# Loading one weight matrix row by row over the 16 DMA engines: a different split of w_out, and more of it on GpSimd's queue

## The chip, the cores and the metric

The kernel runs on one core of a Trainium2 chip. The metric is the device time of one execution in microseconds, the median of the runs shown. Lower is better. The core has a matrix engine (TensorE, "PE"), VectorE ("DVE"), ScalarE ("ACT"), GpSimd ("POOL") and SyncE ("SP"), and 16 DMA engines that carry every transfer between memory and the core's SBUF. [...]

## The reference

```
x  = A_x                                   # 4 tokens x 640, bf16
xn = layernorm(x)
# attention, one new token per batch entry, 32 heads of 128, cache of 4096 positions
q  = xn @ wq                               # 640 x 4096
p  = softmax(q . k_cache / sqrt(128))      # k_cache: 4 x 32 x 4096 x 128
A  = (p . v_cache) @ wo                    # 4096 x 640
# gMLP, F = 1728, so Fh = 864
z  = gelu(xn @ w_in)                       # 640 x 1728
z1 = z[:, :864];  z2 = layernorm(z[:, 864:])
B  = (z1 * (w_sp * z2 + b_sp)) @ w_out     # w_out: 864 x 640
out = x + A + B
```

The two caches hold 134 MB each; w_out holds 864 rows of 1280 bytes, 1.1 MB.

## The kernel before

**Attention.** The 32 heads are four groups of 8; with 4 batch entries there are 16 "units" of K and 16 of V, each 128 partitions x 65,536 bytes. All of them pass through one SBUF tile `kv` of five slots, each half a unit wide. `seq` (line 148) sets the order K0 K1 K2 K3 V0 K4 V1 K5 ... V15, `place` (154) the two slots of each unit, and `load_unit` (174) issues one transfer (two for a K unit that ends a group). SP issues them in that order (lines 181 and 189), each as soon as the slots that it overwrites have been read. K2, for instance, goes to slots 2 and 3; slot 3 holds the first half of K0 until it has been transposed.

For a K unit `emit_K` makes eight steps: VectorE transposes 128 x 2048 words from `kv` into `w_words` (line 425, two alternating buffers), and TensorE multiplies from there (436). After the fourth unit of a group there is a softmax; `emit_V` (503) multiplies a V unit (509).

**gMLP.** It runs while the first K unit is on its way. Of the 864 rows of w_out a part lies in `w_out`, a tile of 128 partitions x `FA` chunks of one row each, and the rest in `w_rest`, a view of `w_words` (line 129) with `FR` chunks, of which only some partitions are filled; VectorE zeroes it first (128). `PC` (61) lists the pieces of the rest: first and last partition, rows per partition, and k. `load_piece` (131) loads a piece with the source rows ordered so that its leading dimension has k entries. Pieces 0 and 1 are issued by SP (139, 140), piece 2 by POOL, behind a small transfer `walk` (141) whose data nobody uses; `tc.issue_after` (142) fixes that order. The columns of w_in are picked in the same order as the rows of w_out, so the z values land in the partition and chunk where their row of w_out lies (lines 317 to 361: matmuls into `z_ps` and `zr_ps`, then Gelu into `zT`). Then follow the layernorm, the gate and a transposition (to 390), and `FC = FA + FR` chunks x 2 halves of matmuls of line 403, which accumulate in `proj`. TensorE executes in program order, so its K matmuls stand behind those of line 403; and since `w_rest` and the buffers of line 425 are the same words, VectorE's first K transposition waits until line 403 has read them.

**The end.** After V15 come the last pieces of wo (189), the rest of the output projection (552) and two stores.

Of the kernel before, what the change touches and what calls it, by code (L numbers as in the profile page):

```python
# [1 line left out]

# [9 lines left out]
F32 = mybir.dt.float32  # L12
BF16 = mybir.dt.bfloat16
# [3 lines left out]
def kernel(  # L17
# [19 lines left out]
    nc = tc.nc  # L37
    P = 128
    B, Sq, D = A_x.shape
    _, H, Sk, Dh = A_k_cache.shape  # L40
    assert Sq == 1 and B == 4 and Dh == P and D % P == 0
    DC = D // P
# [11 lines left out]
    G = HG * B  # L54
    F2 = B_w_in.shape[1]
    Fh = F2 // 2
    FA = 3
    FR = 17
    nf = FA * P

    PC = ((0, 20, 10, 5), (32, 44, 12, 3), (60, 68, 17, 2))
    f_at = [nf]
    for p0, p1, n, _ in PC:
        f_at.append(f_at[-1] + (p1 - p0) * n)
    assert Fh == f_at[-1]
    FC = FA + FR
    NOUT = A_wo.shape[1]
# [5 lines left out]
    const = ctx.enter_context(tc.tile_pool(name="const", bufs=1))  # L73
# [5 lines left out]
    ps_o = ctx.enter_context(tc.tile_pool(name="ps_o", bufs=2, space=bass.MemoryType.PSUM))  # L79
# [6 lines left out]
    def misc_ps(shape, dtype):  # L86
        misc_ctr[0] += 1
        return ps_m.tile(shape, dtype, tag="misc", name=f"misc{misc_ctr[0]}")
# [5 lines left out]
    n_p = (2 * TC + 1) * 16  # L94
    w_words = const.tile([P, max(2 * NKT + n_p, FR * NOUT // 2)], F32, name="w_words")
    kT_t = w_words[:, 0:2 * NKT].rearrange("p (i n) -> p i n", i=2)
    pT_t = w_words[:, 2 * NKT:2 * NKT + n_p].bitcast(BF16).rearrange("p (j r) -> p j r", r=32)

    def at_slot(i, n, off=0):
        return kv[:, i * SL + off:i * SL + off + n]  # L100
# [22 lines left out]

    w_out = at_slot(2, FA * NOUT, n_in).rearrange("p (c n) -> p c n", c=FA)

    nc.sync.dma_start(out=w_out[:, 0:2], in_=B_w_out[0:2 * P, :].rearrange("(p c) n -> p c n", p=P))
    nc.sync.dma_start(out=w_out[:, 2:3], in_=B_w_out[2 * P:nf, :].rearrange("(p c) n -> p c n", p=P))
    nc.vector.memset(w_words[:, 0:FR * NOUT // 2], 0.0)  # L128
    w_rest = w_words[:, 0:FR * NOUT // 2].bitcast(BF16).rearrange("p (c n) -> p c n", c=FR)

    def load_piece(eng, t):
        p0, p1, n, k = PC[t]
        return eng.dma_start(out=w_rest[p0:p1, 0:n].rearrange("p c n -> p (c n)"),
                             in_=B_w_out[f_at[t]:f_at[t + 1], :].rearrange("(r i c) n -> i r (c n)", i=k, c=n))

    NST = 256
    walk = const.tile([14, NST], BF16)

    load_piece(nc.sync, 0)
    load_piece(nc.sync, 1)  # L140
    sw = nc.gpsimd.dma_start(out=walk, in_=B_w_out[0:14, 0:NST].rearrange("(r i) n -> i r n", i=7))
    with tc.issue_after(sw.ins):
        load_piece(nc.gpsimd, 2)

    NB = 32 * FC
    z_at = n_in + FA * NOUT

# [72 lines left out]
    xnT = const.tile([P, DC, 32], BF16)  # L220
# [43 lines left out]
    for q in range(4):  # L264
        nc.gpsimd.tensor_copy(out=SelE[32 * q:32 * q + 32, :, q % 2, :],
                              in_=b8[32 * q:32 * q + 32, 8:8 + HP, None].to_broadcast((32, HP, P // HG)))
# [10 lines left out]
                          in_=ident_f[:].rearrange("p (q x c) -> p q x c", q=2, c=C2))  # L277
# [12 lines left out]
    for hf in range(NH):  # L290
        nc.tensor.matmul(proj[0:32, 0:NO2], lhsT=ident_bf[:XR, 1 - hf:33 - hf],
                         rhs=x_bf[:, hf * NO2:(hf + 1) * NO2], start=(hf == 0), stop=False)
# [4 lines left out]
    for hf in range(2):  # L297
        for c in range(DC):
            for j in range(NG):
                n0 = j * HG * Dh + hf * 512  # L300
                nc.tensor.matmul(q4_ps[32 * j:32 * j + 32, hf * 512:hf * 512 + 512], lhsT=xnT[:, c, :],  # L301
                                 rhs=wq[:, c, n0:n0 + 512], start=(c == 0), stop=(c == DC - 1))
# [14 lines left out]
    w_z = w_in.rearrange("p c (a f) -> p c a f", a=2)  # L317
    z_ps = misc_ps([P, 2, FA, 32], F32)
    zr_ps = misc_ps([P, 2, 256], F32)


    z_in = [[], [], [], []]
    for t, (p0, p1, n, k) in enumerate(PC):
        src = w_z[:, :, :, f_at[t]:f_at[t + 1]]
        for q in range(p0 // 32, (p1 - 1) // 32 + 1):
            x0, x1 = max(p0, 32 * q), min(p1, 32 * q + 32)
            if x1 - x0 < p1 - p0:
                assert (x1 - x0) * k == p1 - p0
                src_q = src.rearrange("p d a (r i c) -> p d i a r c", i=k, c=n)[:, :, (x0 - p0) // (x1 - x0)]
            else:  # L330
                src_q = src
            z_in[q].append((t, x0 - 32 * q, x1 - 32 * q, src_q))
    z_of = [[sum((x1 - x0) * PC[t][2] for t, x0, x1, _ in z[:m]) for m in range(len(z) + 1)] for z in z_in]
    w_z2 = w_z[:, :, :, 0:2 * P].rearrange("p c a (q j i) -> p c q a i j", q=4, j=32)
    w_z1 = w_z[:, :, :, 2 * P:nf].rearrange("p c a (q j) -> p c q a j", q=4)
    for c in range(DC):
        for q in range(4):
            nc.tensor.matmul(z_ps[32 * q:32 * q + 32, :, 0:2], lhsT=xnT[:, c, :], rhs=w_z2[:, c, q], start=(c == 0), stop=False)
            nc.tensor.matmul(z_ps[32 * q:32 * q + 32, :, 2], lhsT=xnT[:, c, :], rhs=w_z1[:, c, q], start=False,
                             stop=(c == DC - 1))  # L340
        for q in range(4):
            for m, (_, _, _, src) in enumerate(z_in[q]):
                nc.tensor.matmul(zr_ps[32 * q:32 * q + 32, :, z_of[q][m]:z_of[q][m + 1]], lhsT=xnT[:, c, :], rhs=src[:, c],
                                 start=(c == 0 and m == 0), stop=(c == DC - 1 and m == len(z_in[q]) - 1))
    z_f = at_slot(2, 2 * 3 * NB, z_at).bitcast(F32).rearrange("p (a n) -> p a n", a=3)
    z_b = at_slot(2, 2 * NB, z_at + 6 * NB).rearrange("p (a n) -> p a n", a=2)
    zT = z_f[:, 0:2, :].rearrange("p a (i j) -> p a i j", j=32)
    nc.gpsimd.memset(z_f[:, 0:2, :], 0.0)
    nc.scalar.activation(out=zT[:, :, 0:FA, :], in_=z_ps[:], func=ACT.Gelu_apprx_tanh)
    for q in range(4):  # L350
        rows = slice(32 * q, 32 * q + 32)
        for m, (t, x0, x1, _) in enumerate(z_in[q]):
            p0, p1, n, k = PC[t]
            z = zr_ps[rows, :, z_of[q][m]:z_of[q][m + 1]]
            dst = zT[rows, :, FA:FA + n, x0:x1]
            if x1 - x0 < p1 - p0:
                nc.scalar.activation(out=dst, in_=z.rearrange("p a (x c) -> p a c x", c=n), func=ACT.Gelu_apprx_tanh)
            else:
                for a in range(2):
                    nc.scalar.activation(out=dst[:, a].rearrange("p c (i r) -> p c i r", i=k),  # L360
                                         in_=z[:, a].rearrange("p (r i c) -> p c i r", i=k, c=n), func=ACT.Gelu_apprx_tanh)
# [36 lines left out]
    for f0 in range(0, FC, 4):  # L398
        for hf in range(NH):
            for fc in range(f0, min(f0 + 4, FC)):  # L400
# [3 lines left out]
                                 rhs=(w_out[:, fc] if fc < FA else w_rest[:, fc - FA])[:, hf * NO2:(hf + 1) * NO2],  # L404
                                 start=(fc == 1 and hf == 0), stop=False)
# [156 lines left out]
    for i, item in enumerate(seq):  # L562
# [10 lines left out]
        g, b = divmod(u, B)  # L573
# [22 lines left out]
    for c, hf in ((0, 0), (1, 0), (0, 1), (1, 1), (2, 0), (2, 1)):  # L596
        p = min(c, 1)
# [49 lines left out]
```

## Time and profile before

| | us |
|---|---|
| median of 3 runs | 663.58 (663.44 to 665.17) |
| the profiled execution: its span | 661.8 |
| VectorE busy | 377.1 |
| TensorE busy (matmul) | 286.8 |
| ScalarE, GpSimd busy | 74.0, 70.1 |
| bytes read, rate over the span | 282.25 MB, 426 GB/s |

For the profiled execution the profile gives the span alone, from the first to the last instruction; it is 1.8 us below the median of the runs, which time the whole launch. The profile numbers queues: q1 carries what SP issues, q0 what POOL issues, q10 what ACT issues; q8 and q14 fetch instructions. A "packet" is one record of a DMA engine: so many bytes, from when to when. The profile does not name the engine of a packet, but within an engine each packet starts some 3 to 4 ns before the one ahead of it ends, so the 16 chains can be told apart in the records.

### The profile page before, as it was taken

The page shows a single profiled execution, that of the slowest core. Times are in us where ns is not written, and L with a number is a line of the kernel's source. Part 1 is how long each engine was busy: PE and PEld are TensorE (multiplying, and loading weights), DVE is VectorE, ACT ScalarE, POOL GpSimd, SP SyncE. Part 2 cuts the span into 40 slices and gives each one's busy share as a digit, 9 for nine tenths or more (in the row PEclk, how much of TensorE's full clock was granted, in tenths as well). Part 3 has the DMA queues.
Part 4 walks back from the last instruction along what each step waited for, and adds up shares of the span by engine and source line. Part 5 has one row for each costly group of instructions (what it writes and reads, how often), then busy time and mean ns, then how long its engine had stood idle before and what let it go on. Part 6 is the DMA issues. An engine that isn't in the chain of part 4 may idle for free.

```text
span 661.8 us, 5507 instructions
## 1 busy us (share of the span) xinstructions
PE 286.8 (43%) x2291; PEld 107.4 (16%) x2291; DVE 377.1 (57%) x307; ACT 74.0 (11%) x143; POOL 70.1 (11%) x138
## 2 busy tenths in 40 slices
PE   0336555446052456234426065642607245541236
PEld 0221111112011122111102022210202112120113
DVE  5329989766191759718346196764619175971112
ACT  0300000340100000330200000070100000042200
POOL 4620000030200000130300000030110000002300
PEclk9868788669578596676858587665857768766678
DMA  9999999999999999999999999999999999999997
GB/s 370 457 429 428 427 442 437 440 421 428 421 440 433 440 415 446 425 437 436 437 432 432 429 418 437 446 433 440 425 420 436 437 436 417 456 420 437 419 420 289
DMA packets 7132, 282.60 MB, mean 427 GB/s; under 512 B 913, under 2 KB 1308, under 8 KB 1692
## 3 DMA queue, kind: packets, MB, share of 16 engines
q1 hardware_dynamic: 6968, 282.07, 98.9%
q8 instruction: 18, 0.29, 0.2%
q0 software_dynamic: 112, 0.18, 0.1%
q14 instruction: 6, 0.05, 0.0%
q10 hardware_dynamic: 28, 0.01, 0.0%
HBM read 282.25 MB, written 0.01 MB: 426 GB/s over the span
## 4 chain that ended last, share of the span: by engine, by line
DMA 75%; DVE 11%; issue 11%; PE 2%; DVEq 0%; SPq 0%
DMA kv<-in_A_k_cache_dram 59%; DVE w_words L425 11%; DMA kv<-in_A_v_cache_dram 10%; DMA kv<-in_A_wo_dram 4%; DMA kv<-in_A_wq_dram 3%; PE O L509 2%; PE S L436 0%; PE proj L552 0%; DVE o_q L604 0%; DVE o L600 0%; DVEq L425 0%; SPq L189 0%; DVE o_bf L615 0%; SPq L181 0%; PE last L552 0%
## 5 line engine op out<-in xcount | busy, mean ns | idle before, releaser
L425 DVE STREAM_TRANSPOSE w_words<-kv 128x2048 f32<-128x2048 f32 x128 | 282.8, 2275 | 124.8 <-DMA kv<-in_A_k_cache_dram 124.8
L436 PE MATMUL S<-w_words,QZ 128*32 128x512 bf16 x1024 | 186.1, 496 | 258.3 <-DVE w_words L425 258.3
L436 PEld LDWEIGHTS <-QZ 128*32 128x32 bf16 x1024 | 59.7, 110 | 382.9 <-issue 319.5
L509 PE MATMUL O<-kv,Zb 128*32 128x512 bf16 x1024 | 75.0, 458 | 57.4 <-DMA kv<-in_A_v_cache_dram 50.8
L473 ACT ACTIVATE Zb<-w_words,MkE 32x128 bf16<-32x128 bf16 x120 | 61.0, 508 | 117.9 <-PE O L509 104.2
L518 DVE TENSOR_TENSOR om<-O,Mk 128x512 f32<-128x512 f32 x15 | 10.4, 692 | 94.6 <-PE O L509 94.6
L471 POOL TENSOR_SCALAR Zb<-w_words,MkE 32x128 bf16<-32x128 bf16 x60 | 43.1, 718 | 139.3 <-PE O L509 126.9
L509 PEld LDWEIGHTS <-Zb 128*32 128x32 bf16 x1024 | 34.0, 113 | 98.4 <-issue 70.3
L485 ACT ACTIVATE p_bf<-S,negmax 128x1024 bf16<-128x1024 f32 x4 | 4.5, 1114 | 401.8 <-DVE negmax L453 401.8
L469 DVE TENSOR_SCALAR Zb<-w_words,MkE 32x128 bf16<-32x128 bf16 x76 | 24.7, 325 | 2.3
L411 POOL COPY QZ<-qT 32x32 bf16<-32x32 bf16 x16 | 5.0, 315 | 186.4 <-PE S L436 185.9
L519 DVE TENSOR_REDUCE R<-om 128x128 f32<-128x512 f32 x15 | 15.3, 1020 | 0.5
L496 POOL TENSOR_SCALAR rs<-MkB,rowsum 128x4 f32<-128x4 f32 x4 | 1.2, 296 | 112.4 <-ACT p_bf L485 112.4
L491 DVE STREAM_TRANSPOSE w_words<-p_bf 128x1024 bf16<-128x1024 bf16 (+1 forms) x8 | 9.6, 1241 | 5.9 <-ACT p_bf L485 4.1
L542 POOL MEMSET oT<- 128x66 bf16 x4 | 0.5, 146 | 96.5 <-PE proj L552 96.5
L443 DVE TENSOR_REDUCE m<-S 128x1 f32<-128x1024 f32 x4 | 4.9, 1224 | 6.1 <-PE S L436 6.1
L521 DVE TENSOR_SCALAR R<-O,Mk 128x128 f32<-128x128 f32 x1 | 0.4, 351 | 14.0 <-PE O L509 14.0
L531 PE MATMUL misc<-R,SelX 128*128 128x512 f32 x8 | 4.5, 644 | 7.2 <-DVE R L519 5.5
L301 PE MATMUL q<-kv,xnT 128*32 128x512 bf16 x40 | 4.3, 617 | 6.4 <-DVE xnT L222 6.4
L498 PE MATMUL misc<-rs,SelE 128*128 128x4 f32 x8 | 2.4, 365 | 10.4 <-POOL rs L496 10.4
L128 DVE MEMSET w_words<- 128x5440 f32 x1 | 4.6, 4592 | 1.9 <-issue 1.9
L534 DVE TENSOR_TENSOR om<-misc,h 128x512 f32<-128x512 f32 x4 | 2.8, 692 | 4.9 <-PE misc L531 4.9
(107 smaller groups left out, 88.2 us busy)
## 6 DMA issues: line engine op xcount, KB each, us to landing
kv<-in_A_k_cache_dram SPq DMA_DIRECT2D x8, 4096.0 KB, 30.2
kv<-in_A_v_cache_dram SPq DMA_DIRECT2D x1, 6144.0 KB
kv<-in_A_wq_dram SPq DMA_DIRECT2D x1, 5120.0 KB, 16.8
kv<-in_A_wo_dram SPq DMA_DIRECT2D x3, 1280.0 KB
kv<-in_B_w_in_dram SPq DMA_DIRECT2D x1, 2160.0 KB, 22.3
kv<-in_A_v_cache_dram SPq DMA_DIRECT2D x1, 2048.0 KB
kv<-in_A_wo_dram SPq DMA_DIRECT2D x1, 640.0 KB, 23.6
kv<-in_B_w_out_dram SPq DMA_DIRECT2D x1, 320.0 KB
```

The lines of the kernel that those rows point to most:

```text
L128: nc.vector.memset(w_words[:, 0:FR * NOUT // 2], 0.0)
L411: nc.gpsimd.tensor_copy(out=QZ[r0:r0 + 32, :, :, :, 8 + 8 * hp], in_=qT[32 * g:32 * g + 32, NE * hp:NE * hp + NE].rearrange("p e a b -> p ...
L425: nc.vector.transpose(kT.rearrange("p (t r) -> p t r", r=32), kw)
L436: nc.tensor.matmul(S_ps[32 * q:32 * q + 32, i], lhsT=QZ[:, b, 2 * kh + w, e, w0:w0 + 32], rhs=kb[:, i, :, e, :, w], start=(b == 0 and k < ...
L443: nc.vector.tensor_reduce(out=m1[:], in_=S_ps[:].rearrange("p i t m -> p (i t m)"), axis=AX.X, op=ALU.max)
L469: nc.vector.tensor_scalar(out=dst, in0=src, scalar1=mk, scalar2=None, op0=ALU.mult)
L471: nc.gpsimd.tensor_scalar(out=dst, in0=src, scalar1=mk, scalar2=None, op0=ALU.mult)
L473: nc.scalar.activation(out=dst, in_=src, func=ACT.Copy, scale=mk)
L491: nc.vector.transpose(pT_t[:, j0:j1, :], blocks)
L509: nc.tensor.matmul(O_ps[32 * q:32 * q + 32, :, :], lhsT=Zb[b % 2][:, w].rearrange("p h c -> p (h c)"), rhs=vv[:, w * 4 * Dh:(w + 1) * 4 * ...
L518: nc.vector.tensor_tensor(out=om4[:], in0=O_ps[:], in1=Mk4[:, :, None].to_broadcast((P, 4, Dh)), op=ALU.mult)
L519: nc.vector.tensor_reduce(out=R, in_=om4[:].rearrange("p c d -> p d c"), axis=AX.X, op=ALU.add)
```

## The change

FA falls from 3 to 1 and FR from 17 to 12, so the gMLP has 13 chunks instead of 20. 128 rows go to all 128 partitions. The other 736 lie in seven pieces: two of 20 partitions (k = 5) on SP's queue, one of 8 partitions (k = 2) and four of 4 partitions (k = 1) on POOL's queue. For k = 1 the source rows are ordered `(j i) n -> i j n` with i = 3 (pieces of 12 rows per partition) or 11 (pieces of 11), so that neighbouring rows of a partition are not neighbours in memory: each 1280-byte row stands by itself. POOL issues nine transfers in a fixed order, each `issue_after` the one before: walk of 14 rows, piece 2, walk of 12, piece 3, walk of 14, pieces 4 and 5, walk of 12, piece 6. A walk moves 512 bytes per row. The z matmuls of POOL's pieces go to a third PSUM tile `zx_ps`.

```diff
-    FA = 3
-    FR = 17
+    FA = 1
+    FR = 12
     nf = FA * P
 
-    PC = ((0, 20, 10, 5), (32, 44, 12, 3), (60, 68, 17, 2))
+    PC = ((0, 20, 12, 5), (32, 52, 11, 5), (60, 68, 12, 2), (92, 96, 12, 1), (28, 32, 11, 1), (96, 100, 11, 1),
+          (124, 128, 11, 1))
+    NHW = 2
...
-    nc.sync.dma_start(out=w_out[:, 0:2], in_=B_w_out[0:2 * P, :].rearrange("(p c) n -> p c n", p=P))
-    nc.sync.dma_start(out=w_out[:, 2:3], in_=B_w_out[2 * P:nf, :].rearrange("(p c) n -> p c n", p=P))
+    nc.sync.dma_start(out=w_out, in_=B_w_out[0:nf, :].rearrange("(p c) n -> p c n", p=P))
...
+    def fold(n):
+        return 3 if n % 3 == 0 else n
+
     def load_piece(eng, t):
         p0, p1, n, k = PC[t]
-        return eng.dma_start(out=w_rest[p0:p1, 0:n].rearrange("p c n -> p (c n)"),
-                             in_=B_w_out[f_at[t]:f_at[t + 1], :].rearrange("(r i c) n -> i r (c n)", i=k, c=n))
+        src = B_w_out[f_at[t]:f_at[t + 1], :]
+        if k > 1:
+            src = src.rearrange("(r i c) n -> i r (c n)", i=k, c=n)
+        else:
+            src = src.rearrange("(j i) n -> i j n", i=fold(n))
+        return eng.dma_start(out=w_rest[p0:p1, 0:n].rearrange("p c n -> p (c n)"), in_=src)
 
     NST = 256
-    walk = const.tile([14, NST], BF16)
-
-    load_piece(nc.sync, 0)
-    load_piece(nc.sync, 1)
-    sw = nc.gpsimd.dma_start(out=walk, in_=B_w_out[0:14, 0:NST].rearrange("(r i) n -> i r n", i=7))
-    with tc.issue_after(sw.ins):
-        load_piece(nc.gpsimd, 2)
+    walk = const.tile([14, 4 * NST], BF16)
+    walks = [0]
+
+    def load_walk(k):
+        at = walks[0] * NST
+        walks[0] += 1
+        return nc.gpsimd.dma_start(out=walk[0:2 * k, at:at + NST],
+                                   in_=B_w_out[0:2 * k, 0:NST].rearrange("(r i) n -> i r n", i=k))
+
+    for t in range(NHW):
+        load_piece(nc.sync, t)
+    sw = None
+    for step in (("w", 7), ("p", 2), ("w", 6), ("p", 3), ("w", 7), ("p", 4), ("p", 5), ("w", 6), ("p", 6)):
+        with (tc.issue_after(sw.ins) if sw is not None else nullcontext()):
+            sw = load_walk(step[1]) if step[0] == "w" else load_piece(nc.gpsimd, step[1])
...
+    zx_ps = ps_o.tile([P, 2, 256], F32, tag="O", name="zx")
...
+            if k == 1:
+                src_q = src_q.rearrange("p d a (j i) -> p d a i j", i=fold(n))
...
-            if x1 - x0 < p1 - p0:
+            if k == 1 or x1 - x0 < p1 - p0:
                 nc.scalar.activation(out=dst, in_=z.rearrange("p a (x c) -> p a c x", c=n), func=ACT.Gelu_apprx_tanh)
```

More of the change, by code (lines that the diff above doesn't have):

```diff
@@ L1 @@
-from contextlib import ExitStack
+from contextlib import ExitStack, nullcontext
 import concourse.bass as bass
@@ L331 @@
                 src_q = src
+            if k == 1:
+                src_q = src.rearrange("p d a (j i) -> p d a i j", i=fold(n))
             z_in[q].append((t, x0 - 32 * q, x1 - 32 * q, src_q))
-    z_of = [[sum((x1 - x0) * PC[t][2] for t, x0, x1, _ in z[:m]) for m in range(len(z) + 1)] for z in z_in]
-    w_z2 = w_z[:, :, :, 0:2 * P].rearrange("p c a (q j i) -> p c q a i j", q=4, j=32)
-    w_z1 = w_z[:, :, :, 2 * P:nf].rearrange("p c a (q j) -> p c q a j", q=4)
+    z_at_q = []
+    for z in z_in:
+        used = [0, 0]
+        z_at_q.append([])
+        for t, x0, x1, _ in z:
+            w, b = (x1 - x0) * PC[t][2], int(t >= NHW)
+            z_at_q[-1].append(((zr_ps, zx_ps)[b], used[b], used[b] + w, used[b] == 0))
+            used[b] += w
+        assert max(used) <= 256
+    w_z1 = w_z[:, :, :, 0:nf].rearrange("p c a (q j) -> p c q a j", q=4)
     for c in range(DC):
         for q in range(4):
-            nc.tensor.matmul(z_ps[32 * q:32 * q + 32, :, 0:2], lhsT=xnT[:, c, :], rhs=w_z2[:, c, q], start=(c == 0), stop=False)
-            nc.tensor.matmul(z_ps[32 * q:32 * q + 32, :, 2], lhsT=xnT[:, c, :], rhs=w_z1[:, c, q], start=False,
+            nc.tensor.matmul(z_ps[32 * q:32 * q + 32, :, 0], lhsT=xnT[:, c, :], rhs=w_z1[:, c, q], start=(c == 0),
                              stop=(c == DC - 1))
@@ L342 @@
             for m, (_, _, _, src) in enumerate(z_in[q]):
-                nc.tensor.matmul(zr_ps[32 * q:32 * q + 32, :, z_of[q][m]:z_of[q][m + 1]], lhsT=xnT[:, c, :], rhs=src[:, c],
-                                 start=(c == 0 and m == 0), stop=(c == DC - 1 and m == len(z_in[q]) - 1))
+                zt_ps, o0, o1, lead = z_at_q[q][m]
+                last_of = m == len(z_in[q]) - 1 or z_at_q[q][m + 1][3]
+                nc.tensor.matmul(zt_ps[32 * q:32 * q + 32, :, o0:o1], lhsT=xnT[:, c, :], rhs=src[:, c],
+                                 start=(c == 0 and lead), stop=(c == DC - 1 and last_of))
     z_f = at_slot(2, 2 * 3 * NB, z_at).bitcast(F32).rearrange("p (a n) -> p a n", a=3)
@@ L353 @@
             p0, p1, n, k = PC[t]
-            z = zr_ps[rows, :, z_of[q][m]:z_of[q][m + 1]]
+            zt_ps, o0, o1, _ = z_at_q[q][m]
+            z = zt_ps[rows, :, o0:o1]
             dst = zT[rows, :, FA:FA + n, x0:x1]
-            if x1 - x0 < p1 - p0:
+            if k == 1 or x1 - x0 < p1 - p0:
                 nc.scalar.activation(out=dst, in_=z.rearrange("p a (x c) -> p a c x", c=n), func=ACT.Gelu_apprx_tanh)
```

## The prediction

> **What bounds the kernel now.** I read the page first: its slices, its queues, its chain.
>
> ```profile
> span 661.8 us, 5507 instructions
> DMA  9999999999999999999999999999999999999997
> q1 hardware_dynamic: 6968, 282.07, 98.9%
> q0 software_dynamic: 112, 0.18, 0.1%
> DMA 75%; DVE 11%; issue 11%; PE 2%; DVEq 0%; SPq 0%
> ```
>
> In every slice but the last the 16 DMA engines are at least nine tenths busy, almost wholly for SP's queue q1. So only two things move the time: how long the most loaded engine needs, and time in which engines have nothing to fetch. The rest matters only through these.
>
> Next the chain in order of time, around the third K unit (columns: start, us, what), and the timelines of VectorE and of TensorE there.
>
> ```profile
> 17.55 27.97 DMA kv<-in_A_k_cache_dram
> 45.74 2.37 DVE w_words L425 x2
> 54.76 29.47 DMA kv<-in_A_k_cache_dram
> ```
>
> ```profile
> 45.74 17.66 DVE L425 STREAM_TRANSPOSE w_words<-kv 128x2048 f32<-128x2048 f32 x8 [7.52 <-DMA kv<-in_A_k_cache_dram]
> 65.00 17.66 DVE L425 STREAM_TRANSPOSE w_words<-kv 128x2048 f32<-128x2048 f32 x8 [1.60 <-DMA kv<-in_A_k_cache_dram]
> ```
>
> ```profile
> 38.28 0.70 PE L403 MATMUL proj<-kv 128*8 128x320 bf16 x3 [7.41 <-DVE kv L390]
> 39.06 4.06 PE L403 MATMUL proj<-w_words,kv 128*8 128x320 bf16 x33
> ```
>
> K0 lands at 45.5 and its transpositions start at once; K2 is issued at 54.76, when the first half of K0 has been read. The gMLP's last matmuls end at 43.1, 2.6 us before those transpositions, which write over w_rest. The packet records give the other side of the margin: the engines end K1 between 59.6 and 64.4, and K2 between 78.9 and 83.8. So the loading of w_out is hidden only as long as line 403 ends near 45; if it ends later, K0's transposition, K2's issue and at last the DMA engines wait.
>
> Last, the issues on POOL's queue (KB each, us to landing).
>
> ```profile
> w_words<-in_B_w_out_dram POOLq DMA_DIRECT2D x1, 170.0 KB, 12.2
> walk<-in_B_w_out_dram POOLq DMA_DIRECT2D x1, 7.0 KB, 7.9
> ```
>
> 170 KB take 12.2 us beside q1. The records say why. Piece 2 is 8 packets of 21,760 bytes, four on each of two engines; they start at 11.63, 13.94, 16.26 and 17.07, with one 40,960-byte packet of q1 (1.51 us) between neighbours while wq lasts. The walk is 7 packets of 1024 bytes on seven engines: two rows of 512 bytes, not adjacent in memory, travel as one. Every engine that has no data in a transfer of POOL gets as many dummy packets instead, of 4 or 8 bytes, and all 16 a completion of 4 bytes: 7 + 9 + 8 + 14 x 4 + 2 x 16 = 112, which is q0's count above. Dummies too go out one by one, each after a packet of q1. So a transfer on POOL's queue costs a turn per packet on all 16 engines, however small, and a turn is as long as q1's next packet: 1.51 us (wq), 0.64 (w_in), 2.42 (K).
>
> **The change part by part.**
>
> *Compute.* 26 matmuls of line 403 for 40: at 4.84/40 = 0.12 us each, 1.7 less. 416 columns for 640 in the gate's chain (lines 371 to 390, 10 us in all) save some 3 us, four more Gelus of 0.27 to 0.31 cost 1.2. All of it lies ahead of K0's landing: nothing in the sum, 3 us more of margin. The memset of line 128 (4.59 us for 5440 words) shrinks to 3.2 and releases POOL's pieces at 5.2 instead of 6.5.
>
> *Issues.* SP issues one transfer less ahead of K0; q1 has work queued to 21 us then, so nothing. POOL issues nine transfers for two at 0.57 to 0.80 each: eight from 5.2 to about 11, ahead of its next needed step (line 211 at 12.88): nothing. If that cover went, each us late would shift xn, q and K1's issue (25.1), which has 15 us before K0 has gone through.
>
> *Bytes per engine.* Rows beyond the bulk are 24 on all engines before, plus 88 on three, 40 on two, 68 on two, none on nine; after it they are 8, plus 92 on eight. A row costs 47 ns in large packets (808 ns for 17), 52 as a packet of its own. The most loaded engine goes from 112 rows to 100: -0.57 us. What it leads to is in rival 1, since the next term outweighs it.
>
> *Turns on POOL's queue.* A walk takes 2 turns, piece 2 takes 4 + 1. For the pieces with k = 1 no row shows the packets: 48 or 44 rows of 1280 bytes, apart in memory, 12 or 11 adjacent once written. Bounds: one packet per partition, as in piece 2 (4 each, 33 turns in all), or one per row (48 and 44, 197 turns). The walk is the nearest row, being the only one with small pieces apart in memory, and it joins two: 24 + 3 x 22 packets, 4 completions, 13 other turns, 107 in all. I take that. [...]
>
> Against these stand q1's packets from about 10 us, when the pieces are first seen (piece 2's were 4 us after its issue): 4 of wq, 8 of w_in, 8 of w_out, K0's 8, K1's 8 and 5 completions, 41 turns, used up when K1 ends. K2 cannot be issued before K0 is transposed, so then POOL's queue has the engines to itself: some 66 packets, 10 ns for a dummy, 0.1 us for two rows. The last piece lands at about 63.8 (K1's last engine, 0.6 earlier than now) + 1.6 = 65.4. Anything above some 45 turns gives nearly the same, as q1 runs dry at K1 in any case.
>
> *What waits.* Line 403 waits for the last piece, with the K matmuls behind it on TensorE; 25 matmuls x 0.12 = 3.0, so K0's transpositions start at 68.4 instead of 45.74: 22.7 late. K2 is issued at 54.76 + 22.7 = 77.5. Engines that stood idle when V1 was issued (134.90) worked again at 138.1 to 139.1, 3.2 to 4.2 later; at the kernel's start it was 1.6 to 2.8. I take 3.0: 80.5. K2 takes 8 x 2.42 = 19.3, so it ends at 99.8, not 83.8: +16.0. After that VectorE, at 17.5 us a unit against 19.35, stays ahead of the engines, but lost transfer time doesn't come back.
>
> Starting together, the engines lose their differences of rows. What separates them later are instruction fetches: 18 packets of 16 KB on q8, about 39 us apart, on eight engines in turn, each putting its engine back 1.5 us; two each after K2 make 3.0. In the profiled execution the engine that is last at K2 stays last and loses 0.5. So the end shifts by 16.0 + 3.0 - 0.5 = **18.5 us**: the profiled execution's 661.8 becomes 680.3, and its 663.58 median 682.1. Landing 64 to 67, restart 1.6 to 4.2, and line 425 released by part of line 403 (1 us sooner) give 678 to 686.
>
> **The rivals.**
>
> *1. The pieces travel in few packets, and the load decides (not slower).* With 4 packets per piece there are 33 turns, and the last piece lands between 25 and 44; up to about 45 nothing waits, which is the point from which it decides. For: piece 2 moves partition by partition, and these rows are adjacent when written. Against: they are apart when read, as the walk's. Then the ends of the engines count. In the records they are 657.3, 657.7 and 658.1 (88 rows), 655.6 and 657.9 (40), 656.1 and 656.5 (68), 653.9 (none, no fetch) and 656.0 to 657.9 (none, two or three fetches). The change adds -0.6, +1.7, +0.4, +3.6 to 4.0 (should this be the eighth) and -0.8. The last engine would then be that of 40 rows that ends at 657.9 now, because three 8 KB instruction fetches hit it: 659.6, +1.5, a time of 665.1. If those fetches fall elsewhere it is 657.6 to 657.9, -0.4 at best: 663.2. More is not to be had: the mean of the ends is 656.8, so perfect balance gives 1.3.
>
> *2. Something between.* With some 36 to 45 turns, or with a piece on the wrong engine, line 403 ends between 47 and 65. The last engine needs K2 at 63.8, and K2 comes 9 us of transposition and 3 of restart after line 403, so it loses time for each us past 52: 1 to 12 us, 664.6 to 676.
>
> *3. The change doesn't do what it says:* the k = 1 pieces spread over four engines. The leading dimensions of the loads before (5 of 20 partitions, 3 of 12, 2 of 8, 7 of 14) gave 5, 3, 2 and 7 engines; 3 and 11 have no divisor with 4, so one engine. If not, turns fall to rival 1's and its time holds within 2 us.
>
> **How the numbers follow.** Late landing 0.62; rivals 1 and 3 0.30, of which 0.26 within 0.3% (2.0 us, about what a measurement of this kernel can tell from no change), 0.02 faster and 0.02 slower; rival 2 0.08, slower. Faster 0.02, same 0.26, slower 0.72. The likeliest case gives 682.1, its own range 678 to 686. For 8 in 10 the range must reach down to the upper half of rival 1: 664.3 to 686.
>
> **What would show it.** In the changed profile: some 350 to 380 packets on q0 for each k = 1 piece (dummies included) and 1700 in all; a landing of POOL's last piece some 50 us after its issue; VectorE idle from 36 to 68 ahead of line 425, with line 403 waiting on DMA; a slice or two of the DMA row near 65 to 80 well below 9; from K2 on the same pace. Wrong, if q0 shows about 33 packets per engine (some 530) and line 403 ends before 45: then the span is within 2 us of 661.8.

## The result, and the profile after

The changed kernel takes 681.73 us (median of 5 runs, 681.21 to 682.93) where the kernel before takes 663.58 us: a ratio of 1.0273, 95% interval 1.0260 to 1.0286. The forecast was 682.1 us. The profiled execution has a span of 679.7 us, 17.9 more than before.

The page of the changed kernel, in the lines that answer to those of before (span, share of the DMA engines in 40 slices, queues, chain that ended last):

```profile
span 679.7 us, 5493 instructions
...
DMA  9996499999999999999999999999999999999996
...
q1 hardware_dynamic: 6834, 281.89, 96.4%
q0 software_dynamic: 992, 0.39, 0.2%
...
DMA 65%; DVE 13%; issue 13%; another core or an unknown queue 4%; PE 3%; ACT 1%; POOL 1%; SPq 0%; DVEq 0%; ACTq 0%; POOLq 0%
```

Two slices of the DMA row, the fourth and the fifth (51 to 85 us), have fallen to 6 and 4. All other slices but the last are full, as before. The loss is one gap near the start; afterwards the kernel runs at the old pace. q0 has 992 packets for 112, and the chain has a new 4%.

The timeline of TensorE (start, duration, what, and in brackets the idle time ahead of it and what ended that), then VectorE's, SP's and the chain in order of time:

```profile
37.05 0.43 PE L431 MATMUL proj<-kv 128*8 128x320 bf16 x1 [5.76 <-DVE kv L418]
66.40 0.69 PE L431 MATMUL proj<-w_words,kv 128*32 128x320 bf16 x3 [28.92 <-DMA w_words<-in_B_w_out_dram]
66.62 0.47 PE L431 MATMUL proj<-kv 128*8 128x320 bf16 x1
66.88 3.15 PE L431 MATMUL proj<-w_words,kv 128*8 128x320 bf16 x21
```

```profile
68.47 48.36 DVE L453 STREAM_TRANSPOSE w_words<-kv 128x2048 f32<-128x2048 f32 x22 [31.48 <-PE proj L431]
```

```profile
77.49 17.77 SPq L197 DMA_DIRECT2D kv<-in_A_k_cache_dram  x3
```

```profile
37.48 28.88 another core or an unknown queue
68.47 2.37 DVE w_words L453 x2
```

Line 431 is line 403 of before, 453 is 425. The first matmul of line 431 needs only the bulk of w_out and runs at 37.05. The next one waits 28.92 us for a transfer into `w_words`, a piece on POOL's queue; the chain calls the same 28.88 us an unknown queue. The other matmul that needs only the bulk stands behind these in the program and runs at 66.62. VectorE stands for 31.48 us behind line 431. K2 is issued at 77.49, where before it was at 54.76.

The issues on POOL's queue show which transfer it is (KB each, median us to landing), and the windows of before and of after what it does to the DMA engines (stretch, busy time of five engines, then the granted clock, DMA share and GB/s):

```profile
w_words<-in_B_w_out_dram POOLq DMA_DIRECT2D x3, 55.0 KB, 56.4
w_words<-in_B_w_out_dram POOLq DMA_DIRECT2D x1, 120.0 KB, 12.8
```

```profile
45.00:65.00 20.00, 11.73 (x64) 3.69 (x64) 17.66 (x9) 0.00 (x0) 0.00 (x0) 0.74 1.03 446
65.00:84.00 19.00, 11.03 (x64) 3.54 (x64) 17.66 (x8) 0.00 (x0) 0.00 (x0) 0.82 0.96 417
```

```profile
45.00:65.00 20.00, 0.00 (x0) 0.00 (x0) 0.00 (x0) 0.00 (x0) 0.00 (x0) 0.50 0.86 363
65.00:84.00 19.00, 12.67 (x75) 4.60 (x76) 15.53 (x8) 0.00 (x0) 0.00 (x0) 0.68 0.31 118
```

From 45 to 65 us no compute engine does anything, while the DMA engines finish K1. From 65 to 84 us they move 118 GB/s for 417.

The packet records say how the pieces travelled: 45 packets of 5120 bytes (12 + 11 + 11 + 11), that is four rows of 1280 bytes in one, all of a piece on one engine; 8 of 15,360 for piece 2; 26 of 1024 for the walks; 913 dummies and completions of 4 to 16 bytes. 992 / 16 = 62 turns on each engine. The last of them ends at 65.8 us. (The records' own clock starts 10.4 to 10.7 us ahead of the span, by run; times here are in the span's.)

### The profile page after: what moved, and what is told of

It is laid out like the page before. It is cut to its first block, busy times and chain, and to the rows that moved or that the text cites. A ratio compares the mean times of both kernels' runs of the same rounds, so it can differ in the third digit from the quotient of the medians.

```text
span 679.7 us, 5493 instructions
## 1 busy us (share of the span) xinstructions
PE 283.4 (42%) x2277; PEld 106.5 (16%) x2277; DVE 375.1 (55%) x307; ACT 74.5 (11%) x147; POOL 73.4 (11%) x145
## 3 DMA queue, kind: packets, MB, share of 16 engines
q1 hardware_dynamic: 6834, 281.89, 96.4%
## 4 chain that ended last, share of the span: by engine, by line
DMA 65%; DVE 13%; issue 13%; another core or an unknown queue 4%; PE 3%; ACT 1%; POOL 1%; SPq 0%; DVEq 0%; ACTq 0%; POOLq 0%
DMA kv<-in_A_k_cache_dram 53%; DVE w_words L453 12%; DMA kv<-in_A_v_cache_dram 5%; DMA kv<-in_A_wo_dram 3%; DMA kv<-in_B_w_in_dram 3%; PE O L537 1%; PE proj L431 0%; DVE w_words L519 0%; PE S L464 0%; POOL kv L415 0%; DVE Zb L497 0%; ACT L376 0%; DVE m L471 0%; ACT p_bf L513 0%
## 5 line engine op out<-in xcount | busy, mean ns | idle before, releaser
L537 PE MATMUL O<-kv,Zb 128*32 128x512 bf16 x1024 | 72.5, 445 | 59.0 <-DMA kv<-in_A_v_cache_dram 52.5
L501 ACT ACTIVATE Zb<-w_words,MkE 32x128 bf16<-32x128 bf16 x120 | 60.9, 507 | 113.1 <-PE O L537 100.0
L546 DVE TENSOR_TENSOR om<-O,Mk 128x512 f32<-128x512 f32 x15 | 10.4, 691 | 93.2 <-PE O L537 93.2
L431 PE MATMUL proj<-w_words,kv 128*8 128x320 bf16 (+1 forms) x24 | 3.6, 470 | 28.9 <-DMA w_words<-in_B_w_out_dram 28.9
L431 PEld LDWEIGHTS <-kv 128*8 128x8 bf16 (+1 forms) x26 | 1.8, 123 | 36.4 <-issue 29.2
L526 PE MATMUL misc<-rs,SelE 128*128 128x4 f32 x8 | 2.4, 364 | 10.7 <-POOL rs L524 10.7
```

The source lines that it names most:

```text
L431: nc.tensor.matmul(proj[r0:r0 + nb, 0:NO2], lhsT=uT[:, u0:u0 + nb], rhs=(w_out[:, fc] if fc < FA else w_rest[:, fc - FA])[:, hf * NO2:(hf ...
L501: nc.scalar.activation(out=dst, in_=src, func=ACT.Copy, scale=mk)
L537: nc.tensor.matmul(O_ps[32 * q:32 * q + 32, :, :], lhsT=Zb[b % 2][:, w].rearrange("p h c -> p (h c)"), rhs=vv[:, w * 4 * Dh:(w + 1) * 4 * ...
L546: nc.vector.tensor_tensor(out=om4[:], in0=O_ps[:], in1=Mk4[:, :, None].to_broadcast((P, 4, Dh)), op=ALU.mult)
```

## The experiments

The theory on record was that a packet on POOL's queue costs a turn on all 16 engines, behind one packet of SP's queue each, and that too many turns make the last piece late. The rivals: the nine transfers, the 13 chunks or the new rows per engine are the cost; or few turns and no loss. Each run stands beside runs of the kernel before on the same chip, 663.53 to 663.58 us. All of them in one table; turns are packets of q0 / 16, "q0 ends" is the end of its last packet in the records, "K0 read" is the start of the first K transposition on VectorE:

| kernel | turns | q0 ends | K0 read | us |
|---|---|---|---|---|
| before | 7 | 18.6 | 45.74 | 663.58 |
| changed | 62 | 65.8 | 68.47 | 681.73 |
| four pieces with k = 4 | 21 | 28.5 | 53.57 | 673.01 |
| one k = 1, three k = 4 | 32 | 44.9 | 52.91 | 671.81 |
| two k = 1, two k = 4 | 42 | 65.8 | 68.33 | 682.51 |
| before + five k = 1 | 72 | 70.8 | 74.47 | 688.92 |
| pieces of 16 partitions | 22 | 23.5 | 45.94 | 665.76 |
| before + 4 loads, neighbours | 15 | 29.4 | 54.87 | 672.89 |
| before + 4 loads, four apart | 15 | 25.7 | 50.53 | 668.17 |
| before, joining of rows | 27 | 24.8 | 46.54 | 664.53 |
| changed, K0 in small packets | 62 | 37.6 | 40.38 | 667.70 |
| before + two k = 1 | 33 | 25.5 | 46.74 | 664.97 |
| before + three k = 1 | 48 | 60.9 | 64.18 | 678.68 |

### Fewer turns: k = 4 for k = 1

```diff
-          (92, 96, 12, 1), (28, 32, 11, 1), (96, 100, 11, 1), (124, 128, 11, 1))
+          (92, 96, 12, 4), (28, 32, 11, 4), (96, 100, 11, 4), (124, 128, 11, 4))
```

> The four pieces with k = 1 get k = 4 and stay on GpSimd's queue, in the same partitions, the same order, between the same walks; all 736 rows are still loaded. Each piece is then 4 packets of 12 or 11 adjacent rows on four engines instead of 11 or 12 packets on one. Theory (a transfer on GpSimd's queue costs a turn per packet on all 16 engines): 8 turns for the walks, 5 for piece 2, 2 for each of the other four, 21 in all instead of 62. SP's queue has 20 packets per engine before the first K unit, so the last piece lands between 27 and 33 us, line 431 does not wait past 40, the first K transposition starts near 45.7 and the time is 663 to 665.5 us; some 330 packets on q0. Rival (the cost is in the nine transfers as such, in the 13 chunks or in the new rows per engine): nothing of that is changed, 678 to 683 us.

Measured 673.01 us, ratio 1.0141 (1.0124 to 1.0158): neither. The turns are 21, as counted, and line 431 no longer waits for a piece; it ends at 46.4. But half the loss stays, by another way. VectorE's timeline, the windows, and two windows of before:

```profile
53.57 17.66 DVE L453 STREAM_TRANSPOSE w_words<-kv 128x2048 f32<-128x2048 f32 x8 [10.95 <-DMA kv<-in_A_k_cache_dram]
```

```profile
16.00:20.00 4.00, 0.52 (x8) 0.37 (x12) 1.84 (x5) 0.00 (x0) 3.54 (x14) 1.00 0.99 248
20.00:24.00 4.00, 3.08 (x40) 1.26 (x33) 0.69 (x1) 0.14 (x1) 3.79 (x13) 1.00 1.39 367
24.00:28.00 4.00, 0.00 (x0) 0.00 (x0) 1.25 (x1) 0.44 (x1) 2.15 (x12) 0.68 0.92 244
```

```profile
16.00:20.00 4.00, 2.24 (x24) 0.90 (x28) 1.63 (x5) 0.00 (x0) 3.64 (x14) 1.00 0.96 411
20.00:24.00 4.00, 2.54 (x51) 1.12 (x45) 1.22 (x2) 0.59 (x1) 3.79 (x13) 1.00 1.28 540
```

What VectorE now waits for is K0 itself, 7.8 us late. From 16 to 20 us the DMA engines are busy (0.99) and deliver 248 GB/s, where before it was 411. In the records every packet from 16.7 to 19.6 us is slow, on all engines: w_in's 17,280 bytes take up to 2.41 us for 0.64. It begins as the piece for partitions 92 to 95 starts, a packet on each of four engines, and returns with the next two pieces.

### Some pieces with k = 1

The same edit, for the last three pieces and for the last two.

> As the changed kernel, but only the first of the four small pieces (12 rows per partition) keeps k = 1; the other three get k = 4. Theory: 21 + 11 = 32 turns. SP's queue gives 28 up to the end of the first K unit (45.5 us) and then one per 2.4 us, so the last piece lands near 55, the first K transposition starts near 57, and of the changed kernel's loss of 18 us the 11 us go by which that is earlier than 68.5: about 670 us (667 to 673). If turns are not taken one for one with SP's packets, but a piece with k = 1 simply needs its own time (a few us), the loss is a quarter of 18 or less and does not depend on what SP's queue holds: 664 to 668.

> The first two small pieces keep k = 1, the last two get k = 4. Theory: 42 turns, as many as SP's queue has packets per engine up to the end of the second K unit (41), so the last piece lands between 60 and 64, the first K transposition starts between 62 and 66, and the time is 675 to 679 us: three quarters of the loss with two of the four pieces. If each piece with k = 1 costs the same, half of the loss: 672.5.

With one piece 671.81 us (1.0120, 1.0100 to 1.0140), with two 682.51 (1.0281, 1.0259 to 1.0303).

With 32 turns q0 ends at 44.9, ten us sooner than I expected: I had counted SP's 28 data packets up to the end of K0, but not its completions, nor the two turns of the first walk, which pass before the others queue up. Line 431 ends at 49.1, before K0 is there at 52.9; the loss of 8.3 us is again that of slow packets (259 and 272 GB/s from 20 to 28 us, for 540 and 419 before). With 42 turns q0 ends while the engines end K1, as expected, but at 65.8 instead of 60 to 64: here K1 ends from 61.2 to 68.4 us, in the kernel before from 59.6 to 64.4. So the loss is the whole, not three quarters. That it is again the slow packets that put K1 off is argued, not shown. So these two runs show the step from 32 turns to 42, but not cleanly.

### Turns alone, in the kernel before

Five loads with k = 1 stand ahead of piece 2, behind a walk of 4 rows:

```diff
+    for x in range(5):
+        p0 = 72 + 4 * x
+        with tc.issue_after(sw.ins):
+            sw = nc.gpsimd.dma_start(out=w_rest[p0:p0 + 4, 0:12].rearrange("p c n -> p (c n)"),
+                                     in_=B_w_out[48 * x:48 * x + 48, :].rearrange("(j i) n -> i j n", i=3))
```

> The kernel before, with its own split of w_out, and five transfers more on GpSimd's queue ahead of piece 2: each loads 48 rows with k = 1 into four partitions of w_rest that the gMLP multiplies by zeros, so the output stays the same; the walk has 4 rows instead of 14, so that piece 2 comes to the same two engines. The five carry 307 KB that nobody needs, which by bytes is 2.3 us on five engines at most. Theory: 2 turns for the walk, 13 for each of the five, 5 for piece 2, 72 in all; the last piece lands at 65 to 68, the first K transposition starts at 68 to 72, and the time is 680 to 686 us. Rival (the new split of the rows, the new order of the z columns or the 13 chunks cost the time): none of them is here, 663.5 to 666 us.

688.92 us, 1.0379 (1.0363 to 1.0394), slower than either side said. The rival falls: the old split with 20 chunks loses as much and more when turns are added. That it is 3 us beyond the range comes from the end of K1: piece 2's data are through at 66.9, but one engine ends K1 only at 70.7 (the last one before at 64.4) and has POOL's last 13 small packets still to send, so q0 ends at 70.8. Packets are slow here too: K0's 65,536 bytes take up to 4.5 us for 2.42, and from 20 to 28 us the rate is 350 and 308 GB/s for 540 and 419 before. Why they are slow here, and why that one engine is so late, is not shown.

### What makes packets slow: who writes which partitions

Two guesses were left for the slow packets: several engines writing one group of four neighbouring partitions, or several engines reading neighbouring rows of w_out. The first run replaces the four small pieces by three of 16 partitions (68 to 83 with 4 rows each, 112 to 127 and 96 to 111 with 3), with k = 4, so that each of the four engines of a transfer writes four neighbouring partitions and no two of them write the same four (and the second piece on SP's queue gets 12 rows per partition):

```diff
-    PC = (..., (92, 96, 12, 1), (28, 32, 11, 1), (96, 100, 11, 1), (124, 128, 11, 1))
+    PC = (..., (68, 84, 4, 4), (112, 128, 3, 4), (96, 112, 3, 4))
...
-    for step in (("w", 7), ("p", 2), ("w", 6), ("p", 3), ("w", 7), ("p", 4), ("p", 5), ("w", 6), ("p", 6)):
+    for step in (("w", 7), ("p", 2), ("p", 3), ("w", 15), ("p", 4), ("w", 8), ("p", 5)):
```

> [...] All 864 rows are loaded. Turns: 6 for three walks, 5 for piece 2, 5 for each of the three, 26 in all. Two causes stand after the first four runs: turns on GpSimd's queue, and packets of several engines that write one group of four neighbouring partitions at a time (in the run with k = 4 the packets between 27.4 and 30.3 us took up to 3.7 times their usual time, from the moment that four engines wrote partitions 92 to 95). With both theories: no piece late, hardly a slow packet, the first K unit read from 45 to 46 us, 663 to 665.5 us. If instead it is reading of w_out by many engines at once that slows all packets, this kernel has as much of it as the one with k = 4: K0 near 53, 670 to 674 us. [...]

(The 27.4 to 30.3 us in this text are on the records' clock: 16.7 to 19.6 in the span.) The other two add the same four loads to the kernel before; only the partitions differ:

```diff
+    for x in range(4):
+        with tc.issue_after(sw.ins):
+            sw = nc.gpsimd.dma_start(out=w_rest[72 + 4 * x:76 + 4 * x, 0:12].rearrange("p c n -> p (c n)"),
+                                     in_=B_w_out[48 * x:48 * x + 48, :].rearrange("(r i c) n -> i r (c n)", i=4, c=12))
```

with `w_rest[72 + x:85 + x:4, 0:12]` in the second.

> The kernel before, with four transfers more on GpSimd's queue between its walk and piece 2. Each loads 48 rows of w_out, with k = 4, into four neighbouring partitions (72 to 75, 76 to 79, 80 to 83, 84 to 87), one packet of 15,360 bytes on each of four engines; the gMLP multiplies these rows by zeros. Twelve rows more on every engine are 0.56 us, eight turns more leave piece 2 landing before 35 us. Theory (one group of partitions takes about what one engine delivers, and what is held up there slows the other engines): packets take two to four times their usual time for some 2 us per transfer, the first K unit is ready 2 to 8 us later than 45.7, and the time is 666 to 672 us. Without the theory: 664 to 664.6 us.

> As the run with neighbouring partitions, same rows, engines, packets, order and number of turns, but each of the four transfers goes to partitions that are four apart (72, 76, 80, 84, then 73, 77, 81, 85, and so on), so that no two engines of a transfer write the same group. Theory of the groups: packets at their usual durations, first K unit at 45.7 to 47, 663.8 to 665 us. If the slow packets come from reading neighbouring rows of w_out, or from eight turns and 196 KB more, it is as slow as with neighbouring partitions.

Measured: pieces of 16 partitions 665.76 us (1.0033, 1.0020 to 1.0045), neighbours 672.89 (1.0141, 1.0121 to 1.0162), four apart 668.17 (1.0070, 1.0050 to 1.0091). VectorE's wait for K0 and two windows each, in this order:

```profile
45.94 17.66 DVE L452 STREAM_TRANSPOSE w_words<-kv 128x2048 f32<-128x2048 f32 x8 [9.71 <-DMA kv<-in_A_k_cache_dram]
```

```profile
16.00:20.00 4.00, 1.80 (x20) 0.72 (x24) 2.07 (x5) 0.00 (x0) 3.53 (x15) 1.00 0.98 415
20.00:24.00 4.00, 3.60 (x74) 1.66 (x68) 0.69 (x1) 0.56 (x1) 3.80 (x14) 1.00 1.17 490
```

```profile
54.87 17.66 DVE L429 STREAM_TRANSPOSE w_words<-kv 128x2048 f32<-128x2048 f32 x8 [9.21 <-DMA kv<-in_A_k_cache_dram]
```

```profile
16.00:20.00 4.00, 0.00 (x0) 0.10 (x1) 1.73 (x5) 0.00 (x0) 3.59 (x15) 1.00 1.10 246
20.00:24.00 4.00, 2.83 (x28) 1.21 (x31) 0.00 (x0) 0.00 (x0) 3.79 (x13) 1.00 0.89 248
```

```profile
50.53 17.66 DVE L429 STREAM_TRANSPOSE w_words<-kv 128x2048 f32<-128x2048 f32 x8 [8.72 <-DMA kv<-in_A_k_cache_dram]
```

```profile
16.00:20.00 4.00, 2.03 (x20) 0.77 (x24) 1.84 (x5) 0.00 (x0) 3.59 (x14) 1.00 0.97 298
20.00:24.00 4.00, 2.43 (x24) 0.78 (x17) 0.87 (x2) 0.59 (x1) 3.79 (x12) 1.00 1.18 432
```

Rows, engines, bytes (245,760, not the 196 KB of the expectation) and turns are the same in the last two, so the 4.7 us between them come from the partitions alone. Reading isn't the cause: with pieces of 16 partitions, too, four engines at a time read neighbouring rows, and the packets of w_in take at most 0.67 us. "Four apart" is not as clean as I had expected: no two engines of one transfer write the same four neighbouring partitions there, and yet it takes 4.6 us more than the kernel before. Why is not shown: the records name neither engines nor partitions, so they don't tell who else writes there in w_in and wq. With neighbouring partitions K0 is read 9.1 us late, four apart 4.8, with pieces of 16 partitions 0.2; the time follows, 9.3, 4.6 and 2.2 longer. The 2.2 of the last is not K0's: there nearly all packets have their usual durations, and at the end of the run the mean of the 16 engines' ends is 656.9 for 656.8 before, so together they lose nothing. One engine alone ends late, at 660.0 (the last one before at 658.1), 2 us after all others. In this split five engines (k = 5 in both pieces of SP's queue) have 104 rows each where the mean is 54, and five engines end K1 at 63.8 to 64.5 when the rest are through by 62.3; that the late engine is one of these, set back further by instruction fetches, is argued. By q0's count it was 22 turns, not 26: 3 rows of one partition and 3 of the next went as one packet of 7680 bytes.

How four engines that write four neighbouring partitions slow the others is not shown. In the run with four pieces of k = 4 packets are slow on all engines (up to 2.41 us for 0.64), those that write elsewhere too. That such a group takes about what one engine delivers and so holds up the others, as the expectation for neighbouring partitions has it, was the author's theory; no run shows it by itself.

### How rows are joined to a packet

Two transfers more in the kernel before, of 24 pieces of 2560 bytes and 48 of 512. That they go to an engine's own partitions, as the expectation says, was the author's assumption; no run shows which partitions an engine writes in the big transfers.

```diff
+        sw = nc.gpsimd.dma_start(out=w_rest[52:56, 0:12].rearrange("p c n -> p (c n)"),
+                                 in_=B_w_out[0:48, :].rearrange("(j i s) n -> i j (s n)", i=3, s=2))
...
+        sw = nc.gpsimd.dma_start(out=w_rest[56:60, 0:12, 0:NST],
+                                 in_=B_w_out[48:96, 0:NST].rearrange("(j i) n -> i j n", i=3))
```

> Measures how rows are joined to packets on GpSimd's queue. The kernel before, its walk with 10 rows, and two transfers more ahead of piece 2, each with k = 1 on one engine and to that engine's own four partitions, multiplied by zeros: the first has 24 pieces of 2560 bytes (two rows each), the second 48 pieces of 512 bytes. In the changed kernel four rows of 1280 bytes went as one packet of 5120. If packets close at four pieces, these are 6 packets of 10,240 and 12 of 2048 bytes; if they close once 4096 bytes are reached, 12 of 5120 and 6 of 4096. Turns by the first 2 + 7 + 13 + 5 = 27, by the second 2 + 13 + 7 + 5 = 27; piece 2 lands before 40 us and the time is 663.5 to 665 us either way.

The records have 12 packets of 5120 bytes for the first and 6 of 4096 for the second, so here packets closed at 4096 bytes (eight of 512) and at 5120 (two of 2560). In the changed kernel three rows of 1280, 3840 bytes, did not close one and four, 5120, did; in the run with pieces of 16 partitions 3840 did not and 7680 did. A limit above 3840 and up to 4096 bytes fits all four, an estimate from these sizes. Single stretches of 15,360 bytes (changed kernel) and 21,760 (before) went as one packet each. The time is 664.53 us in its one run.

### Turns alone, in other partitions, and the same turns against small packets

Two runs add k = 1 loads of 48 rows to the kernel before, now into partitions 20 to 23 and 24 to 27, each on one engine, behind a walk of 10 rows: 2 + 13 + 13 + 5 = 33 turns instead of 7. The second adds a load into 56 to 59, behind a walk of 30 rows: 33 + 2 + 13 = 48. The gMLP multiplies these rows by zeros. The third leaves everything of the changed kernel and cuts K0:

```diff
     cuts[("v", NU - 1)] = (0, 192, T)
+    cuts[("k", 0)] = tuple(range(0, T + 1, T // 8))
```

> [...] SP's queue offers 32 on the engines with the fewest packets up to the end of the first K unit, so the last piece lands at 42 to 46, the first K transposition starts at 46 to 49, which the 14 us that K1 still needs cover: 663.5 to 665.5 us. If each turn costs the same wherever it falls (18 us for 55 more turns in the changed kernel), 26 more cost 8.5: 672.

> [...] Theory: the turns beyond 32 go against K1's packets of 2.42 us, which are used up at 60 to 64.4 us; the last piece lands at 61 to 66, the first K transposition starts at 64 to 70, and the time is 676 to 682 us. If each turn costs the same wherever it falls: 41 more cost 13.4, 677, but then 33 turns are 672. If turns alone cost little and the slow packets of engines that write the same group made the loss in the other runs: 663.5 to 666.

> The changed kernel with one edit in SP's part: the first K unit is issued in eight transfers of 32 positions each, so it reaches the engines in packets of 8192 bytes (0.31 us) for 65,536 (2.42 us). GpSimd's transfers, their 62 turns, the pieces, the 13 chunks, line 431 and its wait are as they were. Theory (a packet of GpSimd's queue waits for one packet of SP's queue, whatever its size): the first K unit now offers 72 turns per engine for 9, so all 62 are through while it is being read; the last piece lands before 45 us instead of at 66.4, the first K transposition starts at 45 to 49 us, and the time is 663 to 666.5 us. Rival (the transfers of GpSimd's queue take some 50 us of their own, by time and not by packets of SP's queue): 680 to 683 us.

Measured: 33 turns 664.97 us (1.0015, 1.0004 to 1.0025), 48 turns 678.68 (1.0218, 1.0197 to 1.0238), 62 turns with K0 in small packets 667.70 (1.0052, 1.0035 to 1.0069). VectorE's timeline with 33 turns, TensorE's with 48, then VectorE's and POOL's transfers with K0 cut:

```profile
46.74 17.66 DVE L432 STREAM_TRANSPOSE w_words<-kv 128x2048 f32<-128x2048 f32 x8 [8.59 <-DMA kv<-in_A_k_cache_dram]
```

```profile
37.98 0.70 PE L416 MATMUL proj<-kv 128*8 128x320 bf16 x3 [7.42 <-DVE kv L403]
61.58 0.42 PE L416 MATMUL proj<-w_words,kv 128*8 128x320 bf16 x1 [22.90 <-issue]
```

```profile
40.38 17.66 DVE L454 STREAM_TRANSPOSE w_words<-kv 128x2048 f32<-128x2048 f32 x8 [2.58 <-PE proj L432]
```

```profile
q0 software_dynamic: 992, 0.39, 0.2%
...
w_words<-in_B_w_out_dram POOLq DMA_DIRECT2D x3, 55.0 KB, 24.5
```

Fifteen turns more, from 33 to 48, cost 13.7 us; 26 more, from 7 to 33, cost 1.4. A price per turn is thus refuted: what counts is against which packets of SP's queue the turns fall. With 33 turns VectorE waits for K0 alone, and q0 ended at 25.5, not at 42 to 46; the old split loads its bulk in 16 small packets per engine (two transfers), not 8, and I had counted 8. The time came out right only because either landing is early enough. With 48 the last piece waits for K1's packets (line 416 at 61.58; the profile names no releaser).

The cut run is the plainest: the same 992 packets on q0, and the median landing of the three 55 KB pieces falls from 56.4 to 24.5 us because the packets that they stand behind are 0.31 us instead of 2.42. Nothing waits for a piece any more, and 14.0 of the 18.2 us are back. It stays 4.1 above before, 1.2 beyond the range. Part of it can be seen: K0's packets of 8192 bytes take 0.320 us in the median where the least is 0.309, its last engine ends at 47.6 and K1's at 66.9, 2.5 later than before. In the mean of the engines K1 ends at 63.8 (before 61.3, changed kernel 62.5), and at the end of the run they are 2.2 later than before, the last one 3.8. So 2.5 us are lost by the end of K1, 1.2 of which the changed kernel loses too. How the rest arises stays open.

## Why the prediction was right, and where it was wrong

**The compute, the issues, the memset, counted as hidden:** right. POOL's transfers are issued in time, line 431's first matmul stands ready at 37.05 for 38.28 before, and in the run with pieces of 16 partitions, which has the 13 chunks and the smaller memset too, these matmuls end at 40.0 for 43.1: 3.1 us more of margin, forecast 3. That run comes to 665.76.

**Bytes per engine, -0.57:** invisible, as forecast; the gap outweighs it. The run with pieces of 16 partitions shows something near it, though it deals out the rows differently (up to 104 per engine for 100): without the gap it takes 2.2 us more, no gain, a little above the 663.2 to 665.1 of the first rival. (The prediction's 24 and 8 rows "beyond the bulk" are the bulk itself; the sums are right.)

**Turns, 107:** the mechanism is right, the size wrong. A piece with k = 1 does go through one engine and does cost all 16 a turn per packet, but the walk was a poor row for the joining: it has only two pieces to join. Four rows of 1280 bytes share a packet, 12 + 11 + 11 + 11 packets, 62 turns and 992 packets on q0 in place of 1700. The wrong term cost nothing, since the step after it says that anything above some 45 turns gives nearly the same.

**"Some 45 turns", and 41 up to the end of K1:** right for the new split (42 turns end with K1). It is not a constant: in the old split 33 turns are over at 25.5, as the engines begin K0 (21.7 to 25.5), and with K0 in small packets 62 pass before it is read.

**Landing 65.4, K0 at 68.4, K2 issued at 77.5:** 66.40, 68.47 and 77.49. The last packet ends at 65.8 and line 431 goes on at 66.40, one later than forecast: K1 ended at 65.6 and not at 63.8, with hardly any turns left to run after it. That the packets of POOL's queue, which each engine carries, make K1 late is argued. The transposition starts 2.1 after the landing and not 3.0, ahead of line 431's last matmul. The two misses cancel, which is luck.

**Restart 3.0, K2 ends at 99.8:** the 3.0 is too long. K2's first packets start 1.0 to 2.0 us after its issue in the records and take 2.4 to 3.2 us for 2.42. Fifteen engines end K2 from 98.4 to 99.0; less 19.4 us of packets that is a restart of 1.6 to 2.2. The row that the 3.0 came from was misread: when V1 was issued, at 134.90, all 16 engines were still busy, the first until 137.0. So K2 ends 15.2 later than before (99.0 for 83.8), not 16.0. Only the sixteenth engine ends at 100.3, behind an instruction fetch of 16 KB at 96.4, which belongs to the next term.

**+3.0 for fetches, -0.5:** right. In the V units of the changed kernel each fetch sets its engine back by about 1.55 us, and eight engines get two, one of them the first before K2 is through. 15.2 and 3.1 make 18.3; the span is 17.9 longer, which leaves 0.4 for the 0.5. So the sum of 18.5 is 0.6 above the change of the span, nearly all of it the restart. The ends spread from 1.8 us at K2 to 3.8 in the last V units and 3.7 at the end (672.3 to 676.0), as forecast.

**The rivals.** The third falls with the packets on one engine. The first, few packets and no loss, needed more than few packets: the run with 21 turns takes 673.01, because of slow packets, which the forecast did not have. The second let the loss begin when line 403 ends, and the K transposition starts, at 52 us. In three kernels in which POOL's pieces are late the start of that transposition less the loss is 49 to 50: 64.18 less 15.1, 68.47 less 18.2, 74.47 less 25.4.

## What to carry to other kernels

A small transfer on GpSimd's queue is not hidden because it has few bytes: count its packets on its busiest engine, add the completion, and set that number against the packets that the other queue still has to send before the data are needed, with their durations. Cut the big transfer or join the small pieces until that comes out: here 62 turns ended at 65.8 us against packets of 2.42 us and at 37.6 against packets of 0.31, and 21 turns at 28.5. And look at which partitions the engines of a transfer write: four packets at a time, from four engines into four neighbouring partitions, slowed every engine here (up to 2.41 us for 0.64).

## What the runs showed of the hardware that was not expected

- Four extra transfers of 60 KB cost 9.3 us when each has four engines write four neighbouring partitions, and 4.6 when the partitions are four apart; by their size, 12 rows per engine at 47 ns, it would be 0.56, an estimate from the 808 ns of 17 rows in the kernel before. From 16 to 24 us the DMA share is 0.89 to 1.18 meanwhile, and only GB/s shows it (246 and 298 for 411).
- Rows on GpSimd's queue were joined to packets of 4096 bytes (from 512), 5120 (from 1280 and from 2560) and, beyond the border of a partition, 7680 (three rows of 1280 from each of two).
- That a packet of GpSimd's queue waits for one packet of SP's was expected; that this holds for packets of 8192 bytes as for those of 65,536, the cut run showed: the same 62 turns end at 65.8 us against packets of 2.42 us, and at 37.6 against packets of 0.31.
